# A planned attention and two-MLP kernel: seven products for one more superblock, and accumulating transfers on GpSimd

## The chip, the cores and the metric

The kernel runs on one core of a Trainium2 chip. The time is that of one execution of the whole program on the device in microseconds; "time" is the median over the runs shown. The engines are named as in the profile: PE is TensorE (matmuls), PEld its weight loads, DVE is VectorE, ACT is ScalarE, POOL is GpSimd, and SP issues the transfers (DMAs).

## What is computed

The reference is an attention without a softmax, followed by two MLPs, all in float32. Shortened:

```
B, S, D, d_qk, d_ff = 2, 3008, 256, 64, 2048
attn = maximum(z @ z.T / S, 0) ** 2          # per batch, S x S
x = u * (attn @ v)                           # 6016 tokens x 256
h = x @ w1_in;  g = h - tanh(h);   x = g @ w1_out
h = x @ w2_in;  g = maximum(h, 0) + alpha * minimum(h, 0)
return g @ w2_out
```

The weights of the MLPs arrive as float64 words and are split on the device.

## The kernel before

**Precision by products.** Every float32 operand is split into a rounded high part and a remainder ("high" and "low", both in the fp32r form that the matmul takes). A product of two operands is three matmuls: high by high, low weights by high, high weights by low. ScalarE mostly makes the high part (a cast, L535 through `copy_on`; on VectorE L536), VectorE the low part (a subtraction, L568 in `split`).

**Stages.** The attention works on 12 blocks of up to 512 queries. The MLPs work on six superblocks of 2 x 512 tokens (the last 2 x 448), and inside one on eight units, each with two rows of 128 hidden features (`lo` and `hi`). The order of superblocks is first MLP 0, first MLP 1, second MLP 0, first MLP 2, second MLP 1, and so on. The forward part of the first MLP's superblock 0 lies inside the attention. Each superblock has a forward part (tokens to hidden features, `unit`) and a backward part (hidden features to output, `back`), which lags the forward part by 26 stage steps of 32.

**Seven products or plain.** Most units multiply 2 x 2 blocks of weights and tokens by seven products in place of eight (`stage` in `unit`): sums and differences of weight blocks S1 to S4 are made once for each MLP (`need_sums`), differences of token blocks once for each superblock (`need_x`), and the partial results are put together in PSUM by copies (`copy`) and adds (`plus`, L1025). A superblock below `SEVEN[kind]` is computed plainly instead: `plain_stage` has four products for each unit with two blocks of depth each, 6 matmuls apiece.

**Weight sums.** For each MLP and each half `e`, `need_sums` loads the high and the low part of four weight quarters back from memory (eight loads of 256 KB on SP, L721), adds them on VectorE ("join", L723), makes the four sums (L729), splits these and stores the parts. `SUMS_DUE` says when that is due.

**Element work.** For the first MLP, `finish` makes h - tanh(h) of each hidden row: tanh on ScalarE into `ts`, then `ts = f - ts` on VectorE ("subtract", L992). For small h a series is used: ScalarE makes a factor `gs` (four passes, L984), VectorE multiplies (`f = f * gs`, "series", L995; it reads `f` after the subtract has read it, and waits for `ts`) and picks by a mask (L998). For the second MLP `out` has a Relu on ScalarE (L968) and a VectorE instruction (L970).

**The plan.** The program is not written in the order in which it is built. `Plan` keeps every operation with the engines that may do it, its price on each, what it reads and writes, and a due time counted back from the order of the TensorE products, which is fixed by hand. `Plan.run` then plays the program through: whenever an engine is free it takes the ready operation with the earliest due time for which there is room in the buffers; an operation with two possible engines goes to the one that takes it first, under some rules (`left_to_act`, `in_the_way`, penalties). `improve` repeats that up to 40 times and moves due times ahead where TensorE would have waited. The instructions are emitted in the order of the planned start times, and each engine works through its own list in that order; semaphores hold an instruction until its inputs are there. So a price in the plan sets an order, never a start on the chip. The prices on ScalarE and VectorE are multiplied by `MARGIN`. A transfer's planned end is

```
pipe = max(t + FIXED, pipe) + op.size + ...      # FIXED = 1.9, size in us
op.done = pipe + (0.1 if t < 5.0 else LANDING)   # LANDING = 4.0
```

**Buffers.** 51 slots of 128 x 1024 float32 (55 after the attention's turned blocks are gone) hold all tiles, called `sb` in the profile; eight PSUM banks are called `bank`. All transfers are issued by SP, but for one store at the end on ScalarE.

Of the kernel before, what the change touches and what calls it, by code (L numbers as in the profile page):

```python
# [17 lines left out]
ALU = mybir.AluOpType  # L18
# [21 lines left out]
MARGIN, LANDING, FIXED, FLYING = 1.03, 4.0, 1.9, 8  # L40
W1_DUE, W2_DUE = (40.0, 250.0), (250.0, 450.0)
SUMS_DUE, SUMS_AHEAD = ((500.0, 545.0), (640.0, 680.0)), 60.0
SEVEN = {1: 1, 2: 1}
# [3 lines left out]
ACT_SLACK = 15.0  # L47
PART_AHEAD, X_AHEAD, SPLIT_AHEAD = 22.0, 30.0, 25.0
# [4 lines left out]
PE, ACT, DVE, SP = "PE", "ACT", "DVE", "SP"  # L53
# [77 lines left out]
class Plan:  # L131
# [48 lines left out]
    def set_due(self, t0):  # L180
# [5 lines left out]
        for op in reversed(self.ops):  # L186
            if PE in op.engines:
                op.due = op.nominal
                continue
            end = min([b.due + off for b, off in op.before], default=1e9)  # L190
            if op.limit is not None:
                end = min(end, op.limit())
            op.due = end - op.ahead - self.fastest(op) - op.tail - (op.size + FIXED + 2.0 if SP in op.engines else 0.0)
# [8 lines left out]
    def run(self, cold=5.0, first=1.45):  # L202
        now, seq = 0.0, 0
        events = []
        busy = {PE: first, ACT: 1.0, DVE: 1.0, SP: 0.7}
        ready = {ACT: [], DVE: [], SP: []}
# [29 lines left out]
        def start(op, e, t, us):  # L236
# [4 lines left out]
            if e == SP:  # L241
                pipe = max(t + FIXED, pipe) + op.size + (THIRD if t > 0.7 and len(flying) == 2 and t < 2.0 else 0.0)
                op.done = pipe + (0.1 if t < 5.0 else LANDING)
                flying.append(op.done)
# [3 lines left out]
            push(busy[e], "free", e)  # L248
            if op.name[0] == "seven":
# [51 lines left out]
        def turn(t):  # L301
            nonlocal pe_at
            for e in (ACT, DVE, SP):
# [8 lines left out]
                while j < len(lst):  # L312
# [4 lines left out]
                    if e in coming and in_the_way(op, e, t) or e == DVE and left_to_act(op, t):  # L317
                        j += 1
                        continue
                    if allowed(op, t):  # L320
                        del lst[j]
                        start(op, e, t, op.engines[e] * (1.0 if e == SP else MARGIN))
                        break
# [86 lines left out]
    def penalty(self, op, e, more):  # L410
        if len(op.engines) == 1 or e == ACT:
            return 0.0
# [17 lines left out]
def attention_two_mlps_kernel(  # L430
# [107 lines left out]
    def dma(name, emit, reads=(), writes=(), us=0.7, limit=None, horizon=1e9, holds=()):  # L538
        return add(name, {SP: 0.44}, lambda e: emit(nc.sync), reads, writes, limit=limit, horizon=horizon,
                   tail=0.0, size=us, holds=holds)  # L540

# [168 lines left out]
    def need_sums(kind, e):  # L710
# [6 lines left out]
        for a, kd in A_COLUMNS:  # L717
            x = quarters[a, kd] = ("wf", kind, e, a, kd)
            for j, key in enumerate((x, ("wg", kind, e, a, kd))):
                c = A_COLUMNS[a, kd] + j  # L720
                dma(("load", key), lambda q, c=c, key=key: q.dma_start(out=columns(key), in_=stored(kind, e, c)),  # L721
                    [("w7d", kind, e, c)], [key], us=1.0, horizon=SUMS_AHEAD, limit=finish)
            add(("join", x), {DVE: dve_us(NB)}, lambda _, x=x, key=key: nc.vector.tensor_add(  # L723
                out=f32(x), in0=f32(x), in1=f32(key)), [key], [x], limit=finish)
# [210 lines left out]
    def unit(kind, s, p):  # L935
# [38 lines left out]
        def finish(f):  # L974
# [5 lines left out]
            if kind == 1:  # L980
# [9 lines left out]
                act("tanh", ts, f, AF.Tanh, parts)  # L990
                us = dve_us(n)
                add(("subtract", ts), {DVE: us}, lambda e: nc.vector.tensor_sub(  # L992
# [317 lines left out]
```

## Time and profile before

| | |
|---|---|
| time, median of 3 runs | 1437.55 us (1437.46 to 1439.22) |
| the profiled execution's own time | 1437.61 us |
| its span, first to last instruction | 1435.8 us |
| granted TensorE clock | 1.000 of full speed |
| TensorE busy | 1429.0 us, 6603 matmuls |
| VectorE busy | 1317.8 us, 1611 instructions |
| ScalarE busy | 1224.8 us, 1648 instructions |
| GpSimd busy | 0.2 us, 4 instructions |
| moved by transfers | 290.60 MB, mean 202 GB/s |

Busy time is the union of an engine's instructions. Matmuls are pipelined: one is listed with a duration longer than the distance to the next one's start. VectorE and ScalarE instructions overlap the next one by some 0.1 us as well.

### The profile page before, as it was taken

The numbers are of one execution on the slowest core, as the hardware profiler recorded it, in microseconds if no ns is written. First come the engines' busy times: TensorE is split into PE (matmuls) and PEld (weight loads), VectorE is DVE, ScalarE is ACT, GpSimd is POOL, SyncE is SP. The second block draws the span as 40 slices with busy tenths as digits, with TensorE's granted clock in tenths as the row PEclk, the third lists the DMA queues.
The fourth block names the chain that finished last, engine by engine and source line by source line (L and its number), as shares of the span: only waits on it lengthen the run. The fifth ranks groups of instructions, "written<-read, shape, count | busy, mean of one in ns | idle before, by whom it ended". The sixth has DMA issues, their size and how long they took to land.

```text
span 1435.8 us, 18888 instructions
## 1 busy us (share of the span) xinstructions
PE 1429.0 (100%) x6603; PEld 1188.5 (83%) x6603; DVE 1317.8 (92%) x1611; ACT 1224.8 (85%) x1648; POOL 0.2 (0%) x4
## 2 busy tenths in 40 slices
PE   9999999999999999999999999999999999999998
PEld 6788888788888888888888888888888888888898
DVE  8999987999999999999999999999999999999664
ACT  9985557888997999998999989999999989996442
POOL 0000000000000000000000000000000000000000
PEclk9999999999999999999999999999999999999999
DMA  7899986899768875747555454655555464636430
GB/s 257 236 283 294 298 289 204 268 270 279 256 223 255 278 232 188 242 154 237 175 173 189 124 179 166 198 168 158 164 165 181 131 200 151 209 107 222 141 125 26
DMA packets 203806, 290.60 MB, mean 202 GB/s; under 512 B 24640, under 2 KB 132800, under 8 KB 203712
## 3 DMA queue, kind: packets, MB, share of 16 engines
q1 hardware_dynamic: 203568, 289.28, 63.7%
q8 instruction: 52, 0.85, 0.2%
q14 instruction: 42, 0.34, 0.1%
q10 hardware_dynamic: 144, 0.11, 0.0%
HBM read 215.56 MB, written 73.79 MB: 202 GB/s over the span
## 4 chain that ended last, share of the span: by engine, by line
PE 99%; DMA 0%; ACT 0%; SPq 0%; DVE 0%; issue 0%
PE bank L527 99%; DMA sb<-in_v 0%; ACT sb L535 0%; ACT sb L858 0%; SPq L585 0%; ACT sb L874 0%; PE bank L529 0%; SPq L628 0%; DVE sb L536 0%
## 5 line engine op out<-in xcount | busy, mean ns | idle before, releaser
L527 PE MATMUL bank<-sb,sb 128*128 128x512 f32 (+2 forms) x6456 | 1411.0, 387 | 1.0 <-ACT sb L535 1.0
L527 PEld LDWEIGHTS bank<-sb,sb 128*128 128x128 f32 (+1 forms) x6456 | 1173.0, 188 | 234.7 <-issue 12.5
L984 ACT ACTIVATE sb<-sb 128x1024 f32<-128x1024 f32 (+1 forms) x480 | 478.1, 1041 | 2.6 <-DVE sb L995 1.1
L535 ACT CAST sb<-sb 128x1024 fp32r<-128x1024 f32 (+3 forms) x411 | 385.0, 977 | 30.6 <-DVE sb L970 11.1
L568 DVE TENSOR_TENSOR sb<-sb,sb 128x1024 fp32r<-128x1024 f32 (+2 forms) x276 | 300.5, 1104 | 11.0 <-ACT sb L535 10.3
L535 ACT COPY sb<-bank 128x512 f32<-128x512 f32 (+1 forms) x230 | 130.9, 577 | 49.8 <-PE bank L527 46.7
L968 ACT ACTIVATE sb<-bank 128x512 f32<-128x512 f32 (+1 forms) x152 | 89.6, 589 | 51.0 <-PE bank L527 49.8
L998 DVE COPY_PREDICATED sb<-sb,sb 128x1024 f32<-128x1024 int32 (+1 forms) x96 | 130.9, 1370 | 1.5 <-ACT sb L984 1.5
L970 DVE SCALAR_TENSOR_TENSOR sb<-sb,rest,bank 128x512 f32<-128x512 f32 (+1 forms) x152 | 110.6, 732 | 11.1 <-ACT sb L968 10.5
L995 DVE TENSOR_TENSOR sb<-sb,sb 128x1024 f32<-128x1024 f32 (+1 forms) x96 | 114.8, 1197 | 5.5 <-ACT sb L984 4.9
L992 DVE TENSOR_TENSOR sb<-sb,sb 128x1024 f32<-128x1024 f32 (+1 forms) x96 | 114.7, 1196 | 1.6 <-ACT sb L984 1.6
L858 ACT ACTIVATE sb<-bank 128x512 f32<-128x512 f32 (+1 forms) x162 | 82.7, 622 | 38.4 <-PE bank L527 38.2
L882 DVE TENSOR_TENSOR sb<-sb,sb 128x1024 fp32r<-128x1024 f32 (+2 forms) x88 | 100.7, 1163 | 6.0 <-ACT sb L535 5.9
L1025 DVE TENSOR_TENSOR bank<-bank,sb 128x512 f32<-128x512 f32 (+1 forms) x80 | 54.7, 684 | 27.2 <-PE bank L527 26.0
L896 DVE STREAM_TRANSPOSE flip<-sb 128x512 f32<-128x512 f32 x120 | 76.5, 685 | 0.1
L874 ACT ACTIVATE sb<-sb 128x1024 f32<-128x1024 f32 (+2 forms) x72 | 73.0, 1077 | 0.0
L928 DVE TENSOR_TENSOR sb<-sb,sb 128x1024 fp32r<-128x1024 f32 (+1 forms) x60 | 69.9, 1173 | 1.3 <-ACT sb L535 1.1
L1025 DVE TENSOR_TENSOR sb<-bank,sb 128x512 f32<-128x512 f32 (+1 forms) x80 | 54.0, 675 | 7.7 <-PE bank L527 7.0
L536 DVE COPY sb<-bank 128x512 f32<-128x512 f32 (+2 forms) x51 | 34.2, 672 | 16.7 <-PE bank L527 16.5
L535 ACT COPY bank<-bank 128x512 f32<-128x512 f32 (+1 forms) x67 | 38.5, 574 | 11.3 <-PE bank L527 10.8
L651 ACT ACTIVATE sb<-sb 128x512 int32<-128x512 int32 x32 | 21.3, 667 | 23.1 <-DVE sb L649 23.1
L970 DVE SCALAR_TENSOR_TENSOR sb<-sb,rest,sb 128x512 f32<-128x512 f32 (+1 forms) x40 | 28.8, 733 | 0.0
(36 smaller groups left out, 293.9 us busy)
## 6 DMA issues: line engine op xcount, KB each, us to landing
sb<-w SPq DMA_DIRECT2D x96, 512.0 KB, 4.7
sb<-wo SPq DMA_DIRECT2D x96, 512.0 KB, 4.6
sb<-w SPq DMA_DIRECT2D x80, 384.0 KB, 4.3
flip<-flip SPq DMA_DIRECT2D x100, 256.0 KB, 4.6
sb<-flip SPq DMA_DIRECT2D x40, 512.0 KB, 5.4
w<-sb SPq DMA_DIRECT2D x64, 256.0 KB, 3.0
sb<-flip SPq DMA_DIRECT2D x20, 448.0 KB, 5.4
sb<-in_moe_w_in SPq DMA_DIRECT2D x16, 512.0 KB, 5.7
```

The source lines that it names most:

```text
L527: nc.tensor.matmul(out=bank_tiles[at][:, :n], lhsT=lhsT, rhs=rhs, start=start, stop=stop, **how)
L535: return nc.scalar.copy(out=out, in_=in_)
L568: add(("low", l), {DVE: dve_us(n)}, lambda e: nc.vector.tensor_sub(out=r32(l)[:, o:o + n], in0=f32(src)[:, c0:c0 + n], in1=f32(h)[:, o:o + ...
L858: nc.scalar.activation(out=f32(a)[:, c0:c0 + n], in_=bank(ps)[:, :n], func=AF.Relu, scale=scale)
L882: add(("low", lp), {DVE: dve_us(w)}, lambda engine, c0=c0, w=w: nc.vector.tensor_sub(out=r32(l)[:, c0:c0 + w], in0=f32(a)[:, c0:c0 + w], i ...
L968: add(("relu2", part), {ACT: act_psum_us(m) if from_bank else act_us(m)}, lambda g: nc.scalar.activation(out=f32(f)[:, c0:c0 + m], in_=src ...
L970: add(("leak", part), {DVE: 0.06 + dve_us(m)}, lambda g: nc.vector.scalar_tensor_tensor(out=f32(f)[:, c0:c0 + m], in0=f32(f)[:, c0:c0 + m] ...
L984: add((name, to), {ACT: act_us(n)}, lambda e: nc.scalar.activation(out=f32(to)[:, :n], in_=f32(inp)[:, :n], func=func, **how), reads, [to] ...
L992: add(("subtract", ts), {DVE: us}, lambda e: nc.vector.tensor_sub(out=f32(ts)[:, :n], in0=f32(f)[:, :n], in1=f32(ts)[:, :n]), parts, [ts], ...
L995: add(("series", f), {DVE: us}, lambda e: nc.vector.tensor_mul(out=f32(f)[:, :n], in0=f32(f)[:, :n], in1=f32(gs)[:, :n]), [gs, ts], [*part ...
L998: add(("choose", ts), {DVE: CHOOSE + us}, lambda e: nc.vector.copy_predicated(out=f32(ts)[:, :n], mask=f32(gs)[:, :n].bitcast(I32), data=f ...
L1025: add(("add", to), {DVE: dve_us(m)}, lambda e: nc.vector.tensor_add(out=out(), in0=bank(t)[:, :m], in1=f32(fifth)[:, :m]), reads, [to], **how)
```

## The change

The second MLP's superblock 0 is computed by seven products like the later ones (`SEVEN = {1: 1, 2: 0}`), so its weight sums are due 60 to 80 us earlier. The joins of the weight parts are no longer made by a load and a VectorE add: the high part is loaded by SP, and the low part is added to it by an accumulating transfer that POOL issues. In `finish` the tanh is taken of -h, and `ts = f - ts` becomes `ts = f + ts`; from 650 us of the plan on, POOL may do this add as an accumulating transfer from `f` to `ts`, 512 KB inside the memory that the tiles are in, if the backlog of transfers is short and the result's due time is far enough. The plan gets POOL as a fourth engine; POOL's transfers take part in the same `pipe` as SP's. `MARGIN` goes from 1.03 to 1.0, and the plan also tells ScalarE of Relu work that a score product is about to make ready.

```diff
-MARGIN, LANDING, FIXED, FLYING = 1.03, 4.0, 1.9, 8
+MARGIN, LANDING, FIXED, FLYING = 1.0, 4.0, 1.9, 8
-SUMS_DUE, SUMS_AHEAD = ((500.0, 545.0), (640.0, 680.0)), 60.0
-SEVEN = {1: 1, 2: 1}
+SUMS_DUE, SUMS_AHEAD = ((490.0, 530.0), (560.0, 620.0)), 60.0
+SEVEN = {1: 1, 2: 0}
+POOL_US, SUBTRACT_US = 1.2, 2.4
+BACKLOG, POOL_SLACK = 2.5, 6.0
+POOL_FROM = 650.0
...
-            op.due = end - op.ahead - self.fastest(op) - op.tail - (op.size + FIXED + 2.0 if SP in op.engines else 0.0)
+            op.due = end - op.ahead - self.fastest(op) - op.tail - (op.size + FIXED + 2.0 if apart else 0.0)
...
-            if e == SP:
+            if e in (SP, POOL):
                 pipe = max(t + FIXED, pipe) + op.size + (THIRD if t > 0.7 and len(flying) == 2 and t < 2.0 else 0.0)
                 op.done = pipe + (0.1 if t < 5.0 else LANDING)
-                flying.append(op.done)
+                if e == SP:
+                    flying.append(op.done)
...
+            if op.name[0] == "score":
+                for other, _ in op.before:
+                    if other.unmet == 1 and other.name[0] == "relu":
+                        coming[ACT].append((op.done, other))
...
+                    if e == POOL and DVE in op.engines:
+                        late = max(busy[PE] - self.pe[pe_at].nominal, 0.0) if pe_at < len(self.pe) else 0.0
+                        if t < POOL_FROM or pipe > t + BACKLOG or t + op.size + POOL_SLACK > op.due + late:
+                            j += 1
+                            continue
                     if allowed(op, t):
                         del lst[j]
-                        start(op, e, t, op.engines[e] * (1.0 if e == SP else MARGIN))
+                        start(op, e, t, op.engines[e] * (1.0 if e in (SP, POOL) else MARGIN))
...
+    def accumulate(name, emit, reads, writes, us, **how):
+        return add(name, {POOL: POOL_US}, lambda e: emit(nc.gpsimd), reads, writes, tail=0.0, size=us, **how)
...
-            for j, key in enumerate((x, ("wg", kind, e, a, kd))):
-                c = A_COLUMNS[a, kd] + j
-                dma(("load", key), lambda q, c=c, key=key: q.dma_start(out=columns(key), in_=stored(kind, e, c)),
-                    [("w7d", kind, e, c)], [key], us=1.0, horizon=SUMS_AHEAD, limit=finish)
-            add(("join", x), {DVE: dve_us(NB)}, lambda _, x=x, key=key: nc.vector.tensor_add(
-                out=f32(x), in0=f32(x), in1=f32(key)), [key], [x], limit=finish)
+            c = A_COLUMNS[a, kd]
+            dma(("load", x), lambda q, c=c, x=x: q.dma_start(out=columns(x), in_=stored(kind, e, c)),
+                [("w7d", kind, e, c)], [x], us=1.0, horizon=SUMS_AHEAD, limit=finish)
+            accumulate(("join", x), lambda q, c=c, x=x: q.dma_start(
+                out=columns(x), in_=stored(kind, e, c + 1), accum_op=ALU.add), [("w7d", kind, e, c + 1)], [x], 1.4,
+                limit=finish)
...
-                act("tanh", ts, f, AF.Tanh, parts)
+                act("tanh", ts, f, AF.Tanh, parts, scale=-1.0)
                 us = dve_us(n)
-                add(("subtract", ts), {DVE: us}, lambda e: nc.vector.tensor_sub(
-                    out=f32(ts)[:, :n], in0=f32(f)[:, :n], in1=f32(ts)[:, :n]), parts, [ts], holds=[f])
+
+                def subtract(e):
+                    if e == POOL:
+                        nc.gpsimd.dma_start(out=f32(ts)[:, :n], in_=f32(f)[:, :n], accum_op=ALU.add)
+                    else:
+                        nc.vector.tensor_add(out=f32(ts)[:, :n], in0=f32(f)[:, :n], in1=f32(ts)[:, :n])
+
+                add(("subtract", ts), {DVE: us, POOL: POOL_US}, subtract, parts, [ts], size=SUBTRACT_US, holds=[f])
```

## Rows read from the trace of the kernel before

**Rows 1.** The page: busy time by engine; the chain that ended last.
```profile
PE 1429.0 (100%) x6603; PEld 1188.5 (83%) x6603; DVE 1317.8 (92%) x1611; ACT 1224.8 (85%) x1648; POOL 0.2 (0%) x4
...
PE 99%; DMA 0%; ACT 0%; SPq 0%; DVE 0%; issue 0%
```

**Rows 2.** Busy us of PE, PEld, DVE, ACT, POOL (x instructions); clock; DMA share; GB/s.
```profile
520.00:1160.00 640.00, 640.00 (x2824) 529.49 (x2823) 614.15 (x680) 612.75 (x796) 0.00 (x0) 1.00 0.57 180
650.00:1290.00 640.00, 640.00 (x2856) 535.25 (x2855) 606.47 (x680) 609.18 (x805) 0.00 (x0) 1.00 0.54 170
440.00:680.00 240.00, 240.00 (x1083) 201.11 (x1082) 232.47 (x264) 220.85 (x282) 0.00 (x0) 1.00 0.69 222
```

**Rows 3.** The chain that ended last, longest piece (start, us, what).
```profile
459.80 771.55 PE bank L527 x3428
```

**Rows 4.** The view of rows 2 for 40 us slices.
```profile
160.00:200.00 40.00, 40.00 (x192) 32.76 (x191) 35.98 (x51) 20.90 (x29) 0.00 (x0) 1.00 0.95 311
520.00:560.00 40.00, 40.00 (x178) 33.08 (x177) 39.44 (x42) 39.42 (x51) 0.00 (x0) 1.00 0.70 228
600.00:640.00 40.00, 40.00 (x179) 33.10 (x178) 39.22 (x46) 39.65 (x52) 0.00 (x0) 1.00 0.34 102
```

**Rows 5.** ScalarE busy with L968, the second MLP's Relu, by stretch.
```profile
590.00:680.00 90.00, 19.23 (x32) 1.00 0.60 190
```

**Rows 6.** VectorE busy with L1025, adds of seven-product units, by stretch.
```profile
590.00:679.00 89.00, 0.00 (x0) 1.00 0.60 189
679.00:761.00 82.00, 11.13 (x16) 1.00 0.56 183
```

**Rows 7.** Groups by line and shape: busy us, mean ns of one, idle before.
```profile
L535 ACT CAST sb<-sb 128x1024 fp32r<-128x1024 f32 x290 | 299.2, 1067 | 11.0 <-DVE sb L970 4.2 <-DMA sb<-flip 3.1 <-PE bank L527 3.1
L568 DVE TENSOR_TENSOR sb<-sb,sb 128x1024 fp32r<-128x1024 f32 x188 | 226.4, 1219 | 0.7 <-ACT sb L535 0.5
...
L535 ACT COPY sb<-bank 128x512 f32<-128x512 f32 x189 | 109.5, 588 | 33.7 <-PE bank L527 31.8
...
L1025 DVE TENSOR_TENSOR bank<-bank,sb 128x512 f32<-128x512 f32 x64 | 44.6, 697 | 16.1 <-PE bank L527 15.1 <-ACT sb L984 0.4 <-ACT sb L535 0.4
...
L536 DVE CAST sb<-sb 128x1024 fp32r<-128x1024 f32 x14 | 9.3, 685 | 1.2 <-ACT sb L874 1.2
...
L723 DVE TENSOR_TENSOR sb<-sb,sb 128x512 f32<-128x512 f32 x8 | 5.5, 691 | 0.0
```

**Rows 8.** Instructions in order of time: start us, us; VectorE, then ScalarE.
```profile
619.44 0.69 DVE L729 TENSOR_TENSOR sb<-sb,sb 128x512 f32<-128x512 f32 x1
620.04 0.43 DVE L536 CAST sb<-sb 128x512 fp32r<-128x512 f32 x1
620.38 1.23 DVE L568 TENSOR_TENSOR sb<-sb,sb 128x1024 fp32r<-128x1024 f32 x1
621.51 0.75 DVE L970 SCALAR_TENSOR_TENSOR sb<-sb,rest,bank 128x512 f32<-128x512 f32 x1
...
613.50 1.04 ACT L535 CAST sb<-sb 128x1024 fp32r<-128x1024 f32 x1
614.44 1.05 ACT L984 ACTIVATE sb<-sb 128x1024 f32<-128x1024 f32 x1
615.40 0.58 ACT L968 ACTIVATE sb<-bank 128x512 f32<-128x512 f32 x1
```

**Rows 9.** DMA issues: count, KB each, median us from issue to landing.
```profile
sb<-w SPq DMA_DIRECT2D x96, 512.0 KB, 4.7
...
sb<-flip SPq DMA_DIRECT2D x40, 512.0 KB, 5.4
...
sb<-w SPq DMA_DIRECT2D x32, 256.0 KB, 4.5
```

**Rows 10.** VectorE busy with L992, the subtracts, by stretch.
```profile
590.00:645.00 55.00, 8.53 (x7) 1.00 0.51 161
650.00:1290.00 640.00, 75.82 (x64) 1.00 0.54 170
```

More of the change, by code (lines that the diff above doesn't have):

```diff
@@ L52 @@
 SLOT, ODD_SLOT = 13.33e-3, 16.8e-3
-PE, ACT, DVE, SP = "PE", "ACT", "DVE", "SP"
+PE, ACT, DVE, SP, POOL = "PE", "ACT", "DVE", "SP", "POOL"
 SMALL_C = math.sqrt(34.0 / 29.0)
@@ L189, in set_due @@
                 continue
+            apart = SP in op.engines or op.engines.keys() == {POOL}
             end = min([b.due + off for b, off in op.before], default=1e9)
@@ L204, in run @@
         events = []
-        busy = {PE: first, ACT: 1.0, DVE: 1.0, SP: 0.7}
-        ready = {ACT: [], DVE: [], SP: []}
+        busy = {PE: first, ACT: 1.0, DVE: 1.0, SP: 0.7, POOL: 1.0}
+        ready = {ACT: [], DVE: [], SP: [], POOL: []}
         coming = {DVE: [], ACT: []}
@@ L302, in turn @@
             nonlocal pe_at
-            for e in (ACT, DVE, SP):
+            for e in (ACT, DVE, SP, POOL):
                 if busy[e] > t + 1e-9:
@@ L410, in penalty @@
     def penalty(self, op, e, more):
-        if len(op.engines) == 1 or e == ACT:
+        if len(op.engines) == 1 or e == ACT or POOL in op.engines:
             return 0.0
```

## The prediction

> **What bounds the kernel now.** I read the page first, then the chain of waits, then busy time by stretch, then the shapes that the edits add and remove, and last the order of single instructions. The page shows TensorE busy for the whole span, and a chain that ended last which is 99% TensorE matmuls [rows 1]. A busy TensorE may still be a stalled one, so its rate decides: from 520 to 1160 us, where every product is 512 columns wide, 2824 matmuls (one cut by an edge) fill 640 us, or 640/2823 = 226.7 ns each [rows 2]. The chain has 3428 matmuls in one unbroken piece of 771.55 us [rows 3]. TensorE has no bubbles there; time is gained by fewer products, and lost by anything that makes it wait.
>
> The next thing to see is how little room the two helpers have. From 650 to 1290 us VectorE is busy for 606.47 of 640 us and ScalarE for 609.18, 95% each [rows 2]. Earlier it is tighter: in the 40 us slices at 520 and 600 us ScalarE is idle for 0.58 and 0.35 us, VectorE for 0.56 and 0.78 [rows 4]. The changed units lie partly in that stretch: the second MLP's first superblock has its 32 Relu results between 590 and 680 us [rows 5]. No adds of seven-product units stand there; the superblock behind it has 16 [rows 6].
>
> **The change part by part.**
>
> *Seven products.* A unit of that superblock has 4 plain products of 6 matmuls, 24; by seven it has 7 of 3, 21. Eight units: 24 matmuls fewer, at 226.7 ns 5.44 us off TensorE. The superblock is 512 wide, so the extra columns of a narrow first product don't arise.
>
> *What these units add to the helpers.* Per unit two copies out of PSUM (588 ns), together 9.4 us for ScalarE, and two adds (697), 11.2 us for VectorE. The split of the superblock's input goes from two 1024-wide tiles to three and a half: four 512-wide differences and one 512-wide remainder (5 x 0.69, as the joins) and one 1024 remainder (1.22) on VectorE, 4.7 us, and a cast and a half (1.07) on ScalarE, 1.6 us [rows 7]. Sum 26.9 us. These durations overlap the next instruction, though: an add of 0.69 us is followed after 0.60 us, a difference of 1.23 after 1.13, a cast of 1.04 after 0.94 [rows 8]. With about 0.09 us off each of 40 instructions it is 23 us.
>
> *Joins by accumulating transfer.* Eight VectorE adds of 0.69 us (L723, two forms of one size, one shown) go in each MLP [rows 7], 16 x 0.60 = 9.6 us by that pitch. SP issues 16 loads of 256 KB fewer [rows 9], and POOL issues them as accumulates; SP gets 8 loads of 384 KB for the second half of the seven-product weights. Before 650 us of the plan POOL's queue holds joins alone, so behind a waiting join stand other joins, and behind those the sums. I price them at nothing on the path; the cover is the 60 us by which the sums' loads may run ahead. Without it, a join that lands in twice the 4.5 us of the plain load [rows 9] would hold the weights' first use by 4.5 us, once for an MLP.
>
> *The balance from 440 to 680 us.* VectorE is idle there for 7.5 us and ScalarE for 19.2 [rows 2]: 26.7 us. Needed are 23 - 9.6, and 2 x 5.44 because TensorE ends the stretch earlier: 24.3 us. That would leave 2.4 us of 470, against the 5% idle of later stretches; it goes only if some 20 us slide past 680 us. They can: the back products run 26 of 32 stage steps behind, and 7 subtracts of the first MLP stand between 590 and 645 us [rows 10], when the adds of their superblock have ended [rows 6].
>
> *Subtract on POOL.* Of the 96 subtracts, 64 stand after 650 us (16 in each of four superblocks) [rows 10], each a VectorE pitch of 1.13 us [rows 8]: up to 72 us off VectorE, 18 of them in the superblock behind the tight stretch, which takes up what slides. What it costs: the multiply that reads the result now waits for a transfer in place of its own engine. The plan counts on 1.9 + 2.4 + 4.0 = 8.3 us from issue. No row shows an accumulate. Below, it is a plain 512 KB transfer, 4.7 to 5.4 us to landing [rows 9]; above, twice 5.4 since the destination must be read too, 10.8 us. Between these I take 7.5 us: same bytes written, more to read; that is within the plan. If it is late, VectorE stands at the multiply, behind it the adds out of PSUM, and TensorE waits for their banks.
>
> *Room on the queues.* From 650 to 1290 us the DMA engines are busy for 54% at 170 GB/s [rows 2]; in full use they would move 512 KB in 0.524 MB / 315 GB/s = 1.7 us. Accumulates at 1.7 to 3.3 us, 64 times, lift the share to 0.71, at most 0.87. At 0.95, from 160 to 200 us, TensorE was busy for 40.00 of 40 us [rows 4]. I price this at nothing; without that room each weight load that lands late is as long a wait of TensorE.
>
> *Plan without allowance.* The plan's unpadded prices are 1.135 us for a 1024-wide VectorE difference, 0.948 for an activation, 0.928 for a cast. Measured pitches: 1.13, 0.96 and 0.94 [rows 8]. VectorE keeps to the plan; ScalarE falls behind by 1.3%, 2.1 us over 165 us of a tight pair of superblocks, where it used to run ahead. There a late copy out of PSUM holds TensorE. Below: 0, if idle places absorb it; above: 2.1. I take 1.3 us, once, since in every later superblock ScalarE has idle time to catch up.
>
> *Sum.* 1437.61 (the profiled execution, 0.06 above the median of the runs) - 5.44 + 1.3 = 1433.5 us. The start before the first product and the last copies and stores stay as they are.
>
> *A rule that speaks against it.* POOL issues no transfer in this trace [rows 1], so what VectorE does to one isn't seen; VectorE's 1024-wide cast takes 685 ns where a 1024-wide difference takes 1219, so such casts run at double rate [rows 7]. The Trainium skill, "SBUF — State Buffer" (SBUF: two separate sides), says that during such double-rate copies on VectorE GpSimd can't write the descriptors of its transfers, and tells of one that took about 3100 ns where 620 was its time alone. By that page, an estimate of 2.5 us late on each of 64 transfers is 160 us, against 106 spare (rival B), and the sum would be some 1488 us; no run here shows it yet.
>
> **The rivals.**
>
> *A. The tight stretch doesn't fit.* If buffers keep the 20 us from sliding (each offloaded tile also holds its buffers for some 7 us longer, 8.3 in place of 1.13), the helpers want the idle share that they have elsewhere and get it by TensorE waiting. At half of that share, 2.5% against 0.5%, 2% of 235 us come back, 4.7 us: 1437. For it: the slices at 520 and 600 us [rows 4]. Against: later superblocks carry seven products in both MLPs at 95% [rows 2].
>
> *B. The accumulates land late; slower than before.* Place: VectorE's multiply after each offloaded subtract. VectorE's spare time from 650 to 1290 us is 33.5 idle and 72 relieved, 106 us, over 64 transfers 1.7 us each. It decides beyond 8.3 + 1.7 = 10.0 us to landing. At 10.3 us: 64 x 2.0 - 106 = 22 us, 1455; at the upper bound of 10.8: 54 us, 1487. For it: nothing in the trace prices reading the destination, nor POOL's issue. A double-rate cast that holds POOL up by its own 0.69 us [rows 7] would not decide alone: 64 x 0.69 = 44 us. Against: the plain rows lie 3 us below the plan.
>
> *C. POOL is hardly used.* The plan gives it a subtract only if its use is over 8 us away and the backlog of transfers under 2.5 us. If few qualify, VectorE gets no relief after 680 us, and the slide comes back there as waits, about 2 us more than in A: 1439.
>
> **How the numbers follow.** The forecast has 0.56, A 0.19, B 0.19, C 0.06. 0.2% of 1437.6 is 2.9 us, about what a measurement of this kernel can tell from no change. The forecast's own range is 1432.2 (no new wait) to 1435. Faster by over 0.2%, below 1434.7: nearly all of the forecast and a sixth of A, 0.55. Slower, above 1440.4: B and the upper ends of A and C, 0.24. Between: 0.21. The range from 1431.5 to 1443 leaves out most of B and a little below the floor, 0.19 in all.
>
> **What would show it.** Right: 24 fewer 512-wide matmuls at 226.7 ns; adds of seven-product units also where the second MLP's first superblock runs; on POOL 16 joins and 40 to 64 subtracts; VectorE clearly under 95% after 680 us; accumulates landing within 8.3 us; about 1 us of new TensorE waits between 520 and 680 us. Wrong: VectorE waiting for POOL's transfers by 100 us or more, or over 3 us of TensorE waits. What most likely breaks the prediction is the size of the unseen accumulate.

## The result, and the profile after

| | before | after |
|---|---|---|
| time, median of 6 runs beside each other | 1437.59 us (1437.41 to 1439.22) | 1449.8 us (1446.94 to 1458.9) |
| ratio | | 1.0093 [1.0073, 1.0112] |
| the profiled execution's span | 1435.8 us | 1457.1 us |

The kernel became 12.2 us slower, where 4.1 us faster was forecast, and the time lies above the range. Six runs of the kernel before lie within 1.8 us of each other, those of the changed kernel within 12. Its profiled execution is the longest of the six, 9.1 us above the median, so the trace below shows where the time goes, and medians give the sizes, which for this kernel are good to a few us only.

The page of the kernel after, beside [rows 1]: busy time by engine, and the engines' shares of the chain that ended last.

```profile
PE 1432.5 (98%) x6579; PEld 1185.0 (81%) x6579; DVE 1300.2 (89%) x1616; ACT 1211.8 (83%) x1624; POOL 58.1 (4%) x63
...
PE 21%; DMA 1%; DVE 1%; issue 0%; ACT 0%; DVEq 0%
```

TensorE has 24 matmuls fewer, as the change says, and yet is busy for longer; of its span it is idle for 24.6 us, before for 6.8. The chain no longer is TensorE alone: it begins late, with a transfer. The longer busy time is the slower clock behind a wait, as the next windows show. They are those of [rows 2], in three stretches and one short piece.

```profile
440.00:597.00 157.00, 144.60 (x648) 119.82 (x646) 139.19 (x158) 133.41 (x169) 18.16 (x14) 0.99 0.90 256
597.00:680.00 83.00, 81.00 (x339) 64.87 (x340) 78.97 (x91) 81.05 (x110) 0.00 (x0) 0.96 0.56 180
680.00:1300.00 620.00, 616.96 (x2745) 513.88 (x2744) 562.72 (x647) 579.40 (x757) 37.02 (x43) 1.00 0.71 203
...
597.00:603.50 6.50, 6.10 (x15) 4.83 (x16) 4.22 (x5) 5.88 (x8) 0.00 (x0) 0.54 0.68 222
```

The matmuls that run in a stretch (one cut by its edge is counted too) are the best measure of what it loses, because they count waits and a slow clock alike. From 440 to 680 us 987 run, before 1083 [rows 2]: 96 x 226.7 ns = 21.8 us lost, and from 680 to 1300 us 26 fewer than the 2771 of before, 5.9 us. Less the 5.44 us of the 24 matmuls this is 22.2 us, against 21.3 between the two spans. From 597 to 603.5 us 15 matmuls fill 6.1 us, some 0.4 us each: the granted clock is 0.54, near the lower of its two levels (1.2 GHz), after TensorE had stood for 6.02 us. VectorE is idle for 17.8 of the 157 us before 597, 11%, in the stretch in which the prediction feared for its room.

What it waits for there: of the waits of VectorE, of TensorE and of POOL those that bear on this, as total us, times, longest.

```profile
DVE sb L746 <- DMA sb<-w: 13.6, 5, 6.4
```

```profile
PE bank L541 <- ACT bank L549: 7.0, 3, 6.0
PE bank L541 <- DVE sb L1048: 4.4, 4, 2.0
PE bank L541 <- DVE sb L945: 2.7, 1, 2.7
```

```profile
POOL sb L739 <- issue: 30.0, 5, 7.7
```

L746 is a weight sum (L729 before), and `sb<-w` the joins' accumulating transfers (L739). A sixth wait at L746, of 3.3 us, is put down to "issue" by the profile, but it ends at 540.11 us, and the join before it landed at 540.03. The largest wait in order of time (start, us, instruction, idle time before it and its releaser):

```profile
586.88 0.68 DVE L746 TENSOR_TENSOR sb<-sb 128x512 f32<-128x512 f32 x1
...
593.94 0.69 DVE L746 TENSOR_TENSOR sb<-sb,sb 128x512 f32<-128x512 f32 x1 [6.37 <-DMA sb<-w]
594.55 1.22 DVE L1018 TENSOR_TENSOR sb<-sb,sb 128x1024 f32<-128x1024 f32 x1
...
595.80 1.06 ACT L1001 ACTIVATE sb<-sb 128x1024 f32<-128x1024 f32 x1 [6.57 <-DVE sb L1018]
596.76 0.58 ACT L549 COPY bank<-bank 128x512 f32<-128x512 f32 x1
...
597.40 6.99 PE L541 MATMUL bank<-sb,sb 128*128 128x512 f32 x18 [6.02 <-ACT bank L549]
```

Read it upward. TensorE wanted a bank that ScalarE's copy had to make; the copy stood behind an activation that reads a series product (L1018, L995 before); this product stood on VectorE behind a sum whose join had not landed. VectorE and ScalarE both stood idle for over 6 us here, so neither was short of time: the order of the lists carried one late transfer through three engines.

Why was the join late? POOL's first four joins, and the last three, by start:

```profile
425.69 1.45 POOL L739 DMA_DIRECT2D sb<-w  x1 [425.25 <-DVE sb L670]
431.93 1.32 POOL L739 DMA_DIRECT2D sb<-w  x1 [4.80 <-DVE sb L679]
442.38 1.29 POOL L739 DMA_DIRECT2D sb<-w  x1 [9.14 <-DMA sb<-flip]
447.95 1.31 POOL L739 DMA_DIRECT2D sb<-w  x1 [4.28 <-PE bank L541]
...
568.24 1.30 POOL L739 DMA_DIRECT2D sb<-w  x1 [3.42 <-DVE sb L1018]
577.23 1.29 POOL L739 DMA_DIRECT2D sb<-w  x1 [7.69 <-issue]
582.43 1.30 POOL L739 DMA_DIRECT2D sb<-w  x1 [3.91 <-DVE sb L746]
```

The plan gives a join 1.2 us of POOL, so a group of four may leave within 5 us. On the chip they start 5 to 10 us apart. By the transfers' landing times, which the trace has for each of them, three of the first four landed at 431.67, 442.13 and 447.64, and the next started 0.26, 0.25 and 0.31 us later each time, whatever releaser the profile prints. The same holds in the other three groups of four: one join is in flight at a time. The minimum, median and maximum from issue to landing, first of the joins, then of POOL's adds in `finish` (L1012):

```profile
DMA to landing us min/median/max: 4.4/6.1/11.4
```

```profile
DMA to landing us min/median/max: 4.4/6.3/11.4
```

The adds do overlap in flight: 11 of the 43 start while another is under way. A few are late as well, 5 of 43 by more than the plan's 8.3 us: VectorE's series products wait 4.9 us in all for them, and the chain that ended last begins at one:

```profile
1132.31 11.38 DMA sb<-sb
...
1154.11 98.59 PE bank L541 x445
```

### The profile page after: what moved, and what is told of

It reads as the page before. It is cut to its first block, busy times and chain, and to the rows that moved or that the text cites. A ratio compares the mean times of both kernels' runs of the same rounds, so it can differ in the third digit from the quotient of the medians.

```text
span 1457.1 us, 18984 instructions
## 1 busy us (share of the span) xinstructions
PE 1432.5 (98%) x6579; PEld 1185.0 (81%) x6579; DVE 1300.2 (89%) x1616; ACT 1211.8 (83%) x1624; POOL 58.1 (4%) x63
## 5 line engine op out<-in xcount | busy, mean ns | idle before, releaser
L549 ACT CAST sb<-sb 128x1024 fp32r<-128x1024 f32 (+2 forms) x413 | 387.8, 981 | 38.8 <-DVE sb L987 13.7
L549 ACT COPY sb<-bank 128x512 f32<-128x512 f32 (+2 forms) x217 | 123.3, 579 | 38.5 <-PE bank L541 36.6
L985 ACT ACTIVATE sb<-bank 128x512 f32<-128x512 f32 (+1 forms) x144 | 85.4, 593 | 60.8 <-PE bank L541 57.0
L1018 DVE TENSOR_TENSOR sb<-sb,sb 128x1024 f32<-128x1024 f32 (+1 forms) x96 | 114.5, 1196 | 5.7 <-DMA sb<-sb 4.9
L987 DVE SCALAR_TENSOR_TENSOR sb<-sb,rest,bank 128x512 f32<-128x512 f32 (+1 forms) x144 | 104.9, 731 | 14.8 <-ACT sb L985 14.6
L875 ACT ACTIVATE sb<-bank 128x512 f32<-128x512 f32 (+1 forms) x152 | 79.3, 631 | 35.7 <-PE bank L541 35.4
L1048 DVE TENSOR_TENSOR bank<-bank,sb 128x512 f32<-128x512 f32 (+1 forms) x88 | 60.3, 685 | 25.5 <-PE bank L541 23.8
L1048 DVE TENSOR_TENSOR sb<-bank,sb 128x512 f32<-128x512 f32 (+1 forms) x88 | 59.4, 675 | 13.1 <-PE bank L541 12.9
L1014 DVE TENSOR_TENSOR sb<-sb,sb 128x1024 f32<-128x1024 f32 (+1 forms) x53 | 63.7, 1206 | 8.1 <-ACT sb L1001 8.1
L550 DVE COPY sb<-bank 128x512 f32<-128x512 f32 (+1 forms) x72 | 48.1, 669 | 17.9 <-PE bank L541 17.6
L1012 POOL DMA_DIRECT2D sb<-sb x43 | 37.0, 861 | 673.1 <-ACT sb L1001 322.3
L668 ACT ACTIVATE sb<-sb 128x512 int32<-128x512 int32 x32 | 21.3, 664 | 32.7 <-DVE sb L666 26.1
```

Of the source, the lines that this page charges most:

```text
L549: return nc.scalar.copy(out=out, in_=in_)
L875: nc.scalar.activation(out=f32(a)[:, c0:c0 + n], in_=bank(ps)[:, :n], func=AF.Relu, scale=scale)
L985: add(("relu2", part), {ACT: act_psum_us(m) if from_bank else act_us(m)}, lambda g: nc.scalar.activation(out=f32(f)[:, c0:c0 + m], in_=src ...
L987: add(("leak", part), {DVE: 0.06 + dve_us(m)}, lambda g: nc.vector.scalar_tensor_tensor(out=f32(f)[:, c0:c0 + m], in0=f32(f)[:, c0:c0 + m] ...
L1018: add(("series", f), {DVE: us}, lambda e: nc.vector.tensor_mul(out=f32(f)[:, :n], in0=f32(f)[:, :n], in1=f32(gs)[:, :n]), [gs, ts], [*part ...
L1048: add(("add", to), {DVE: dve_us(m)}, lambda e: nc.vector.tensor_add(out=out(), in0=bank(t)[:, :m], in1=f32(fifth)[:, :m]), reads, [to], **how)
```

## The experiments

The kernels differ in order, engines and space, one also in its products. Medians and ratios are against the kernel before on the same chip. The last columns are TensorE matmuls that run from 440 to 597, 597 to 680 and 680 to 1300 us (one cut by an edge is counted on both sides). In the kernel before, whose TensorE doesn't wait there, they are 717, 368 and 2771; each one missing is 226.7 ns. Without new waits the seven-product kernels would have a span of 1435.8 - 5.44 = 1430.4 us; that and 226.7 ns for each missing matmul gives the spans shown to within 0.5 us, but for the two longest (1.4 and 1.6 us too much).

| kernel | median us | ratio, 95% | span | matmuls |
|---|---|---|---|---|
| after | 1449.8 | 1.0093 [1.0073, 1.0112] | 1457.1 | 648, 339, 2745 |
| joins on VectorE again | 1442.8 | 1.0035 [1.0022, 1.0048] | 1441.0 | 717, 344, 2746 |
| POOL's space 2048 to 3072 | 1438.13 | 1.0004 [0.9994, 1.0013] | 1436.8 | 717, 353, 2757 |
| no adds on POOL | 1448.96 | 1.0074 [1.0050, 1.0097] | 1449.9 | 649, 347, 2767 |
| allowance 1.03 | 1441.13 | 1.0021 [1.0012, 1.0031] | 1439.3 | 715, 332, 2770 |
| space + allowance | 1439.73 | 1.0017 [1.0007, 1.0026] | 1438.1 | 717, 333, 2770 |
| space, no adds on POOL | 1435.33 | 0.9986 [0.9977, 0.9996] | 1433.7 | 717, 353, 2771 |
| space, plain products | 1442.03 | 1.0033 [1.0020, 1.0046] | 1440.5 | 717, 368, 2747 |
| joins planned at 7.0 us | 1436.49 | 0.9994 [0.9984, 1.0004] | 1434.1 | 717, 352, 2770 |
| space, no adds, 6 steps | 1440.18 | 1.0018 [1.0009, 1.0027] | 1438.8 | 689, 359, 2770 |
| nothing on POOL | 1437.84 | 1.0003 [0.9994, 1.0012] | 1435.9 | 717, 344, 2769 |
| space, adds planned late | 1435.42 | 0.9986 [0.9977, 0.9995] | 1434.0 | 717, 354, 2770 |
| space, no adds, spread | 1435.37 | 0.9987 [0.9978, 0.9996] | 1433.4 | 717, 356, 2769 |
| space, adds late, spread | 1435.2 | 0.9985 [0.9976, 0.9993] | 1433.5 | 717, 356, 2770 |
| space, no adds, boundary | 1437.43 | 0.9999 [0.9990, 1.0008] | 1435.3 | 717, 351, 2766 |
| space, adds late, boundary | 1436.18 | 0.9990 [0.9981, 0.9999] | 1434.2 | 717, 352, 2770 |

### Which of the parts

**Joins on VectorE again**, by the loads and adds of before.

```diff
-            accumulate(("join", x), lambda q, c=c, x=x: q.dma_start(
-                out=columns(x), in_=stored(kind, e, c + 1), accum_op=ALU.add), [("w7d", kind, e, c + 1)], [x], 1.4,
+            for j, key in enumerate((x, ("wg", kind, e, a, kd))):
...
+            add(("join", x), {DVE: dve_us(NB)}, lambda _, x=x, key=key: nc.vector.tensor_add(
```

> The changed kernel with the sixteen joins put back as they were before: SP loads both parts, VectorE adds them. All else as in the change. Theory 1 (the joins on GpSimd come one after the other, the weight sums on VectorE wait for them, and the adds out of PSUM wait behind the sums): the waits of about 20 us around 440 to 630 us go, and the time falls to 1432 to 1436 us. Theory 2 (the stretch is too full for seven products): VectorE has 9.6 us more to do there, TensorE waits as long or longer, 1448 to 1455 us. Theory 3 (the adds to -tanh land late): nothing changes before 650 us, 1446 to 1450 us.

**More space for POOL's transfers**: the bytes of each partition that the program sets aside for them, with the same plan. What lies in it, the lists of the transfers' pieces, is called descriptors below.

```diff
-dynamic_dma_scratch_size=2048)
+dynamic_dma_scratch_size=3072)
```

> The changed kernel with its instruction lists untouched, but with 3072 bytes of each partition in place of 2048 for the descriptors of GpSimd's transfers. Theory 1 in its narrow form (a join's descriptors fill the space so far that the next can't be written until the last has landed): two joins are in flight at a time, the second of a group is issued 1.3 to 2 us after the first and not 0.3 us after its landing; a group of four takes 13 to 16 us and not 26; the time falls by 8 to 15 us, to 1433 to 1441 us. If the joins wait for each other for another reason (the loads before them, or the order of GpSimd's list): the distances stay at 5 to 10 us and the time at 1446 to 1450 us. Theories 2 and 3: no change in time.

**No adds on POOL**, with the joins as they are.

```diff
-POOL_FROM = 650.0
+POOL_FROM = 1e9
```

> The changed kernel in which GpSimd makes the joins alone; all 96 additions of h to -tanh(h) stay on VectorE. Theory 1: the waits before 630 us stay, 1445 to 1452 us. Theory 3 (the additions on GpSimd land late and hold VectorE): the waits at 976 and 1147 us go and nothing else comes, 3 to 5 us less than the change, if those waits are the loss. If GpSimd's additions give the room in which the delayed work is caught up (the balance in the prediction): more waits of TensorE after 680 us, 1450 to 1460 us.

**The allowance back.**

```diff
-MARGIN, LANDING, FIXED, FLYING = 1.0, 4.0, 1.9, 8
+MARGIN, LANDING, FIXED, FLYING = 1.03, 4.0, 1.9, 8
```

> The changed kernel planned with the allowance of 3% on ScalarE and VectorE as before. Theory 2 (a plan without allowance is too tight): waits of TensorE go, 1436 to 1443 us. Theory 1: the joins are still one after the other, since the allowance touches no transfer; 1443 to 1455 us, in either direction from the change, and the sums still wait for joins on VectorE.

More space is the clean one: the instructions of every engine stand in the same order as in the changed kernel, and 11.7 us go (the slowest of its ten runs, 1440.66 us, is 6.3 us below the fastest of the changed kernel). Its first four joins, beside those above:

```profile
425.55 2.77 POOL L739 DMA_DIRECT2D sb<-w  x2 [425.11 <-DMA sb<-w]
431.82 1.31 POOL L739 DMA_DIRECT2D sb<-w  x1 [3.50 <-DMA sb<-in_uT]
433.92 1.29 POOL L739 DMA_DIRECT2D sb<-w  x1 [0.79 <-PE bank L541]
```

Two leave back to back, and the third as the first has landed (431.57): two are in flight, the group is out in 8 us, not 22, and the waits at L746 are gone from VectorE's list. So the space held the joins back, not the accumulating as such: with two in flight a join takes longer (median 8.1 us, at most 12.5), and costs less. This run also shows how little lead the sums have: in the same lists, the last sum of each group of four starts 0.4 to 10 us after its last join has landed. Taking the joins off POOL undoes 7 us only: VectorE then has eight more adds for each MLP in the tight stretch (344 matmuls there against 353 with more space), and the rest, behind 680 us, belongs to another plan. Without adds on POOL the waits before 630 us stay; those at 976 and 1147 go, so these are the adds'; its time (1444 to 1452 us in four runs) can't be told from that of the changed kernel. With the allowance the joins go on one by one, but 8.7 us go, and the time lies in the range that was expected of a plan that is too tight. The plan starts the last four joins from 539.69 to 563.13 us, in the changed kernel from 563.54 to 582.43, and VectorE waits at the sums for 1.2 us in all. Whether the allowance is worth something by itself is asked next.

### The allowance, the products, the price

**More space and the allowance**; **more space, no adds on POOL**; **more space, plain products**; **joins at 7.0 us in the plan**, without more space. In this order:

```diff
-MARGIN, LANDING, FIXED, FLYING = 1.0, 4.0, 1.9, 8
+MARGIN, LANDING, FIXED, FLYING = 1.03, 4.0, 1.9, 8
-dynamic_dma_scratch_size=2048)
+dynamic_dma_scratch_size=3072)
```

> The changed kernel with 3072 bytes for GpSimd's descriptors and with the plan's allowance of 3% as before. What is left of the loss with the larger space (6 us of TensorE waits, 3 of them where the second MLP's first seven-product units begin) is then put to the plan. If the missing allowance causes it: the waits shrink to 1 or 2 us, 1432 to 1435 us. If the stretch is simply too full for seven products: the plan itself has to wait there, 1437 to 1442 us.

```diff
-POOL_FROM = 650.0
+POOL_FROM = 1e9
-dynamic_dma_scratch_size=2048)
+dynamic_dma_scratch_size=3072)
```

> The changed kernel with 3072 bytes for GpSimd's descriptors and all additions to -tanh(h) on VectorE. If these transfers are a loss (late ones hold VectorE at 957 and 1130 us): those waits of about 2.5 us go and the time falls from 1438.1 to 1434.5 to 1436 us. If they are the room in which delayed work is caught up: waits after 680 us grow and the time rises to 1440 us or more.

```diff
-SEVEN = {1: 1, 2: 0}
+SEVEN = {1: 1, 2: 1}
-dynamic_dma_scratch_size=2048)
+dynamic_dma_scratch_size=3072)
```

> The changed kernel with 3072 bytes for GpSimd's descriptors, but the second MLP's first superblock by plain products as before; its weight sums are still due at the earlier time. TensorE then has 5.44 us more to do. If the seven products bring the waits at 598 to 607 us: those go, and the time is about that of the kernel before, 1437.5 to 1439 us, so that seven products are worth only 0 to 1 us net. If the waits come from the earlier sums or from the plan without allowance: they stay, and the time is 1440 to 1444 us.

```diff
-        return add(name, {POOL: POOL_US}, lambda e: emit(nc.gpsimd)
+        return add(name, {POOL: 7.0}, lambda e: emit(nc.gpsimd)
```

> The changed kernel with 2048 bytes as in the change; only the plan's price for a join on GpSimd is 7.0 us and not 1.2, so that the plan knows that the next one starts about 7 us later. If the loss is that the plan places the weight sums before their joins have landed: VectorE no longer waits there, the joins still come one after the other, and the time is 1435 to 1440 us. If the serial joins themselves are too slow whatever the order: 1444 us or more.

The allowance makes the kernel with space no faster (1.0017 against 1.0004): its absence costs nothing where the joins land in time. The 8.7 us that it gave back without the space came from the joins' places. Without adds on POOL no matmul is missing from 680 us on:

```profile
597.00:680.00 83.00, 81.37 (x353) 65.37 (x353) 82.82 (x97) 80.79 (x113) 0.00 (x0) 1.00 0.63 203
680.00:1300.00 620.00, 620.00 (x2771) 519.14 (x2770) 600.80 (x680) 589.57 (x777) 0.00 (x0) 1.00 0.52 166
```

What is left is 15 matmuls from 597 to 680 us, 3.4 us. Plain products lose none there, and the helpers have 7.6 and 10 us free:

```profile
597.00:680.00 83.00, 83.00 (x368) 68.71 (x367) 75.37 (x83) 73.02 (x97) 0.00 (x0) 1.00 0.52 169
```

So this loss belongs to the first seven-product units. (Plain, the kernel then loses 24 matmuls behind 680, with 7.4 us of VectorE waits for adds on POOL, so its time fits neither of the two that were expected: the waits went, and yet it took 1442 us.) The last one tests the mechanism from the other side: the space is that of the changed kernel, and the plan alone is told that a join takes 7.0 us of POOL. POOL still issues them some 5 us apart and more, VectorE no longer waits at the sums, and 13.3 us go. Its first and its last join:

```profile
411.50 1.45 POOL L739 DMA_DIRECT2D sb<-w  x1 [411.06 <-DVE sb L677]
...
563.22 1.30 POOL L739 DMA_DIRECT2D sb<-w  x1 [3.55 <-DVE bank L1048]
```

The plan starts the first join 14 us and the last one 19 us earlier than in the changed kernel. So joins one at a time are not too slow as such: what cost the time was a plan, with its order and its starts, that didn't know of their pace. How much of the 13.3 us is the order and how much the earlier start was not tried apart.

### What the adds and the joins are worth

**More space, no adds, the second MLP's tokens 6 steps behind in place of 12**; **nothing on POOL** (joins as in the first experiment); **more space, POOL's adds planned 3.5 us later** (11.8 us from issue). In this order:

```diff
-LAG, SHRINK, LAG_END, X_STEPS = 26, 64, 12, 12
+LAG, SHRINK, LAG_END, X_STEPS = 26, 64, 12, 6
-POOL_FROM = 650.0
+POOL_FROM = 1e9
```

> The changed kernel with 3072 bytes for GpSimd's descriptors, all additions to -tanh(h) on VectorE, and X_STEPS 6 in place of 12, so that 6 back steps fewer are forced ahead of the second MLP's first superblock. Theory 4 (the five waits at 598 to 607 us, 3 us in all, come from the hand-made order: the first six stage steps of that superblock stand without back products between them, and a seven-product unit has copies and adds between its products that a plain unit hasn't): the waits go, 1432 to 1433.5 us. If helpers that are too full cause them: they stay, 1435 to 1436 us. If the tokens then come too late: one new wait of some us at the superblock's start, 1436 to 1442 us.

```diff
-            accumulate(("join", x), lambda q, c=c, x=x: q.dma_start(
...
+            add(("join", x), {DVE: dve_us(NB)}, lambda _, x=x, key=key: nc.vector.tensor_add(
-POOL_FROM = 650.0
+POOL_FROM = 1e9
```

> The changed kernel without any transfer from GpSimd: joins and additions on VectorE as before; seven products, due times and the plan without allowance stay. If GpSimd's joins give the room for the seven products (theory 2 in part): 1438 to 1443 us, with waits between 500 and 700 us. If GpSimd isn't needed: the time of the same kernel with joins on GpSimd and enough descriptor space, 1435 to 1436 us.

```diff
-                op.done = pipe + (0.1 if t < 5.0 else LANDING)
+                op.done = pipe + (0.1 if t < 5.0 else LANDING) + (3.5 if op.name[0] == "subtract" else 0.0)
```

> The changed kernel with 3072 bytes for GpSimd's descriptors, and the plan counting on 11.8 us from issue to landing for an addition on GpSimd in place of 8.3. Theory 3 in small (a few additions land later than planned and hold VectorE at the multiply, 2.8 us in all): those waits go, 1435 to 1436 us. If the additions cost in another way (buffers held longer, transfers in each other's way): no gain, 1437 to 1440 us.

The 6 steps move the loss without an end of it: the waits from 598 to 607 us go, but the tokens come late for the first products (28 matmuls missing before 597), and a slow clock follows. Joins on POOL with space are worth 2.5 us against joins on VectorE (1435.33 and 1437.84). Adds planned at their late end make the loss behind 680 us vanish, 42 adds still on POOL. The median landing of 6.3 us lies within the 8.3 that the plan had before, so it was the tail of the landings that cost the 2.7 us. But the adds gain nothing either: with them 1435.42, without 1435.33.

### The 3 us in the first seven-product units

The order of TensorE's work there has stage steps of a unit in a row without a back product between them, where the second MLP starts. TensorE in the run with space and no adds (start, us, form, count, wait):

```profile
595.70 4.53 PE L541 MATMUL bank<-sb,sb 128*128 128x512 f32 x18
600.79 1.65 PE L541 MATMUL bank<-sb,sb 128*128 128x512 f32 x6 [0.56 <-DVE bank L1048]
602.66 4.10 PE L541 MATMUL bank<-sb,sb 128*128 128x512 f32 x15 [0.22 <-DVE sb L1048]
607.51 2.81 PE L541 MATMUL bank<-sb,sb 128*128 128x512 f32 x11 [0.75 <-DVE bank L1048]
```

**These places spread** over 36 stage steps around the start (without and with adds on POOL, planned late), and **put between units only** (the same two):

```diff
+X_SPREAD = 6
+        k = todo.index((2, 0, 0, 0))
+        for e in range(k - 18, k + 18):
+            goal[e] += round(X_SPREAD * (1 - abs(e - k) / 18))
```

> The changed kernel with 3072 bytes for GpSimd's descriptors and all additions on VectorE, and with the six back steps that are forced ahead of the second MLP's first superblock spread over the 18 stage steps before it, and given back over the 18 behind it, so that at most a third of its stage steps stand without a back product between them. The tokens come as early as before. Theory 4 (the order by hand leaves the first seven-product units without cover): of the 3 us of waits at 598 to 607 us 1 or less is left, 1432.5 to 1434 us. If the helpers are too full there: the waits stay or move by some us, 1435 to 1437 us.

> The same spread with the additions on GpSimd, planned with 11.8 us to landing. Theory 4 and theory 3 in small together: 1432 to 1434 us. If the additions on GpSimd are worth something once they are planned right: lower than the kernel with the spread alone by up to 1 us; if they are worth nothing, the same within 0.5 us.

```diff
+        k = todo.index((2, 0, 0, 0))
+        for e in range(k - 24, k + 24):
+            goal[e] += 6 - ((e - k) // 4 if e >= k else (k - e + 3) // 4)
```

> As the spread version without additions on GpSimd, but each of the six places without a back product lies between the last stage step of one unit and the first of the next. In the spread version the waits stand at five of its six such places, 6.7 us apart, and none at the one that falls between two units. Theory 4 with its place named (inside a unit a product waits for an add that starts when the product before it has ended, and only a back product covers that): no waits of TensorE after 590 us, 1432.5 to 1433.5 us. If full helpers cause the waits: they stay at about 2.5 us wherever the places are, 1435 to 1436 us.

> The same with the additions on GpSimd, planned with 11.8 us to landing. Theory 4: 1432.5 to 1433.5 us. If the additions are worth something: below the version without them by up to 1 us; if they are worth nothing, the same within 0.3 us.

Spread, without adds on POOL, the waits move to the new places and get smaller (the edit moves the lines by one, L1049 is the add of L1048):

```profile
601.40 19.75 PE L542 MATMUL bank<-sb,sb 128*128 128x512 f32 x84 [0.18 <-DVE bank L1049]
621.61 6.46 PE L542 MATMUL bank<-sb,sb 128*128 128x512 f32 x27 [0.46 <-DVE sb L1049]
628.33 6.41 PE L542 MATMUL bank<-sb,sb 128*128 128x512 f32 x27 [0.27 <-DVE bank L1049]
634.93 5.30 PE L542 MATMUL bank<-sb,sb 128*128 128x512 f32 x22 [0.20 <-ACT bank L550]
```

From 597 to 680 us 12 matmuls are missing in place of 15, but the time is the same (1435.37 and 1435.33 us), which is what was expected of helpers that are too full. With the adds planned late it is 1435.2 us, the lowest of all medians and 2.2 us below the kernel before, though no measurement here parts it from the other two. None reaches the 4.1 us that were forecast. Put between units, the waits at those places are gone too, but two others come, and the time was not the 1432.5 to 1433.5 us that was expected:

```profile
595.68 31.01 PE L541 MATMUL bank<-sb,sb 128*128 128x512 f32 x136
628.33 9.13 PE L541 MATMUL bank<-sb,sb 128*128 128x512 f32 x39 [1.63 <-DVE bank L550]
638.85 1.43 PE L541 MATMUL bank<-sb,sb 128*128 128x512 f32 x5 [1.39 <-ACT bank L549]
```

```profile
597.00:680.00 83.00, 79.97 (x351) 65.45 (x351) 82.97 (x100) 78.84 (x110) 0.00 (x0) 1.00 0.59 196
```

VectorE is busy for 82.97 of 83 us there, and both waits are for copies that stood behind other work on VectorE and ScalarE. That would fit an order and a full helper that each hold TensorE by about 3 us, so that removing one shows the other; since every change of the places is also another plan, it isn't shown. How the 3 us divide between them stays open. With the places between units the adds on POOL, planned late, are 1.3 us faster than without them (1436.18 and 1437.43), the only pair in which they gain more than 0.2 us.

## Why the prediction was wrong

The step that failed is the price of the joins: nothing on the path was foretold, and they cost 11.7 us. By medians, one step after the other: 1437.6 - 5.4 (24 matmuls) + 3.1 (waits in the first seven-product units; 1435.33 with space and no adds on POOL) + 2.8 (POOL's adds, late in their tail; 1438.13 with space) + 11.7 (joins one at a time) = 1449.8. The missing matmuls say the same by another way: 15 are 3.4 us, 14 more 3.2, and 95 more 21.5 us in a profiled execution that is 9.1 us above the median. The last term is the least certain: the changed kernel's six runs lie from 8.8 to 20.8 us above the median with more space.

**Seven products: right on TensorE's side, without their waits.** 24 matmuls are gone, and 16 adds stand from 590 to 679 us (L1048) where [rows 6] had none:

```profile
590.00:679.00 89.00, 10.48 (x16) 0.96 0.58 191
```

With space and without adds on POOL the counts and the span agree on 5.4 us less, with 3.4 of new waits at these units: more than the 1.3 us of waits in the forecast, less than rival A's 4.7.

**Joins by accumulating transfer: the step that failed.** It said that joins and sums stand behind a waiting join, "I price them at nothing on the path", with the 60 us of lead as cover, or 4.5 us once for an MLP without it. Two things were wrong. Joins don't follow each other at POOL's 1.2 us but at a landing each, 5 to 10 us, which no row of before could show since POOL issued nothing. And the lead was no cover: it holds for the loads, while on VectorE's list the sum stands just behind where the plan believes its join landed (0.4 to 10 us behind the landing in the run with more space, not 60). What waits behind a sum in VectorE's order (series products, adds out of PSUM) was not named. VectorE stood for 13.6 us in five waits, TensorE waited behind it, and after the longest wait it ran at the lower clock: 11.7 us. The order was the plan's, the joins' pace came from the space; changing either alone brings the time back (3072 bytes, or 7.0 us in the plan).

**Subtract on POOL and rival B.** The accumulate's price was taken well in the middle, 7.5 us against a median of 6.3, but its bounds were those of a mean, and the tail went to 11.4, over the upper bound of 10.8. Rival B had the right kind of mechanism, VectorE held by a late accumulating transfer, at another instruction: at the multiply it was 4.9 us of waits and (with more space) 2.8 us of time, not 22 to 54, and at the sums 11.7. Its point of decision, 10.0 us to landing, was worked out for the mean of 64; here 5 of 43 over the plan's 8.3 us were enough, as there was no room near them.

**The balance and rival A.** The tight stretch doesn't quite fit: some 3 us come back where A said 4.7. The relief after 680 us came: VectorE is busy for 562.72 of 620 us, 91% in place of 95 [rows 2]. It was worth nothing by itself (1435.42 us with it, 1435.33 without), since TensorE had no waits there before. Rival C fell: 43 of the 64 subtracts were on POOL.

**Plan without allowance: priced at 1.3 us, not seen.** With space, 1.03 in place of 1.0 gives nothing back; the 8.7 us that it gives back without the space are the joins' again.

**Room on the queues: right.** The DMA share from 680 to 1300 us rose to 0.71, its forecast lower end, and no transfer is among the releasers of TensorE's waits; those it did set back held VectorE first.

**The rule that speaks against it.** The other sum took 2.5 us late on each transfer, an estimate by the Trainium skill, "SBUF — State Buffer" (SBUF: two separate sides): during double-rate copies on VectorE GpSimd can't write the descriptors of its transfers. The trace of the changed kernel can't tell, since none of POOL's 59 issues overlaps a cast on VectorE; its adds take 856 ns by the minimum and the median, at most 896. Other runs can. Where the joins are on VectorE again, one add takes 1.42 us:

```profile
912.43 1.42 POOL L1012 DMA_DIRECT2D sb<-sb  x1 [4.84 <-ACT sb L1001]
...
913.07 0.69 DVE L550 CAST sb<-sb 128x1024 fp32r<-128x1024 f32 x1
```

The traces of all runs have 447 adds on POOL, and a cast on VectorE overlaps the issue of six. In four of these the cast begins 0.42 to 0.68 us into the issue, and the issue ends 86 to 89 ns after the cast, 0.26 to 0.59 us later than one of 856 ns. In the other two, with the cast at the very start or 0.84 us in, it takes 866 and 856 ns. So VectorE's casts do hold POOL up, but by 0.59 us at most and four times in 447, not by 2.5 us on each. Rival B's own price for this, 0.69 us, was near.

## What to carry to other kernels

When work moves from an engine to a queue, ask three things of the new order: at what pace the queue really issues (not how long an issue takes, but what must be free before the next can start), what stands behind the first reader on that reader's engine, and whether a planner's lead is a lead in the order or only in its due times. Here the plan that was told of the joins' pace lost nothing by it; the one that wasn't put their readers where they blocked. Relief for an engine off the critical path was worth only the waits that it had caused.

## What the hardware showed

- With 2048 bytes set aside for POOL's transfers one 256 KB join was in flight, with 3072 two: the next issue came 0.25 to 0.32 us after a landing. The adds (33 of 512 KB, 10 of 448) overlap at either size. Why joins need more space than adds of twice the bytes was not tried apart; a join is in more and smaller packets, 528 of some 500 bytes against 144 of 3.5 KB for an add, by the packets, MB and share of POOL's queue where it makes 16 joins alone (more space, no adds) and 45 adds alone (joins on VectorE again):

```profile
q0 software_dynamic: 8448, 4.20, 2.4%
```

```profile
q0 software_dynamic: 6480, 23.01, 8.4%
```

- POOL's issue of a join took 1292 to 1445 ns in the changed kernel, that of an add 856 to 896. In the four cases above, a cast on VectorE that began 0.42 to 0.68 us into an add's issue put the end of the issue to 86 to 89 ns after its own end.
- Accumulating adds inside the tile memory landed after 4.4 to 11.4 us, median 6.3, where plain 512 KB loads took a median of 4.7 to 5.4 in the kernel before [rows 9].
- A wait of 6.02 us of TensorE was followed by 6.5 us at a granted clock of 0.54, in which 15 matmuls took 6.10 us and not 3.4: 2.7 us on top of the wait.
